# Gated unit's last weights: from 13 rows on every partition and one row dealt over five DMA engines to 12 rows and two rows dealt in stacks of four

## The chip, the cores and the metric

The kernel runs on one core of a Trainium2 chip. The metric is device time in microseconds (us), the median of several runs of the whole program. The engines are named as in the profile: PE (matrix multiplication; PEld its weight loads), DVE (vector), ACT (scalar), POOL (general), SP (here it issues nearly all transfers). "DMA engine" is one of the core's 16 transfer engines, which carry what SP and ACT issue.

## The reference

One decoding step for a batch of 8 with one token each, width 512. The token is normalised, then goes two ways: through attention over the last 2048 positions of a key and value cache (32 query heads, 8 cached heads of 128), and through a gated unit of width 1792. Both results are multiplied and added to the input.

```python
xn = _layernorm(x)
# A: attention over the last W = 2048 cached positions
q = (xn @ wq) as 32 heads of 128
scores = q . k * 128 ** -0.5 ;  p = softmax(scores) ;  o = p . v
s = o.reshape(B, 1, 4096) @ wo
# B: the gated unit
h = sigmoid(xn @ w_gate) * (xn @ w_up)
g = silu(h @ w_down)
return x + s * g
```

All arrays are bf16. `w_down` has 1792 rows of 512, 1 KB each, 1.79 MB in all. The cache windows are 64 MB, all weights together some 15 MB.

## The kernel before

The kernel is a long stream of loads with the arithmetic beside it. SP's queue loads the input and the weights of the gated unit (`wg_sb`, `wu_sb`), the query weights (`wq_sb`, two loads), `w_down`, then 16 tiles of keys and 16 of values of 2 MB each, alternating, and at the end the five pieces of `wo` (12, 8, 6, 4 and 2 rows on each partition). ACT issues two early loads: half of `wg_sb`, and the input in blocks (`x4_sb`, called `x_sb` in the profile).

What may be loaded when is set by a list and by room. `later` (L107) appends a load, `pump` (L110) issues loads from the head of the list while their pool has room, `free` (L116) gives a buffer back and pumps. There are five buffers of kind "k" (keys, `wq`, `wo`) and four of kind "v" (values, `wg`, `wu`, `w_down`). The order on every engine is the order in which the code is written.

The gated unit's second half multiplies the hidden values `h` by `w_down`. The rows of `w_down` stand on the partitions as `(y r) n -> y (r n)`: partition y holds rows 14y to 14y+13, 14 KB in one piece. Of these, rows 1 to 13 of every partition come in one load of 128 partitions (`wd_sb`, L196, `SD` = 1). Row 0 of each partition, 128 rows in all, comes in three further loads into a tile `wd_part` of 64 partitions (L179 to L192), which POOL sets to zero first (L183): 60 rows to partitions 0 to 19 in three slots each, 60 rows to partitions 32 to 51, and 8 rows to partitions 52 to 59 in one slot. The source of each of these loads has an outermost size of 5, 5 and 4 (`a` in L184 to L190). The tile takes one of the four "v" buffers.

The hidden values must stand on the same partitions as the dealt rows. A selection matrix `sel_part` (L276 to L285, seven small copies on DVE) and three matmuls (L363) move them there, DVE copies the result to `hP_sb` (L371), and the product with `w_down` (L384) then has 13 matmuls on 128 partitions and three on at most 60, summed into four column groups. ACT copies the sums (L394), four matmuls add them up (L397), ACT takes the sigmoid (L407) and DVE the product (L411). Then the attention begins: PE transposes the key tiles (L477), DVE copies them out (L482), scores (L496), softmax, values (L593). The last `wo` rows are multiplied at L729, and DVE's two last operations (L744, L746) precede the store.

The two lines that set where a dealt row goes:

```python
PARTS = ((0, NA, 0, SX, 0, A), (Z, NA, 0, SX, SX * NA, A))
in_=src.rearrange("(y a) n -> a y n", a=a)[:, :, : SD * w.shape[1]],
```

Of the kernel before, what the change touches and what calls it, by code (L numbers as in the profile page):

```python
# [10 lines left out]
def kernel(  # L11
# [13 lines left out]
    nc = tc.nc  # L25
    P = 128
    B, _, D = A_x.shape
    _, Hkv, Sk, Dh = A_k_cache.shape
# [5 lines left out]
    FT = F // P  # L34
# [14 lines left out]
    bf16 = mybir.dt.bfloat16  # L49
# [9 lines left out]
    vpool = ctx.enter_context(tc.tile_pool(name="vpool", bufs=4))  # L59
    ktpool = ctx.enter_context(tc.tile_pool(name="ktpool", bufs=3))  # L60
    ppool = ctx.enter_context(tc.tile_pool(name="ppool", bufs=2))
    consts = ctx.enter_context(tc.tile_pool(name="consts", bufs=1))
# [11 lines left out]
    ps_m = ctx.enter_context(  # L74
        tc.tile_pool(name="ps_m", bufs=1, space=bass.MemoryType.PSUM)
    )
    ctx.enter_context(tc.manual_schedule())


# [1 line left out]
    q0, q1 = nc.sync, nc.scalar  # L81
    k_tiles = {}
    v_tiles = {}
    room = {"k": 5, "v": 4}
    pools = {"k": kpool, "v": vpool}

    def load_cache(cache, tag, b, i):
# [16 lines left out]
    weights = {}  # L104
    todo = []

    def later(tag, f):  # L107
        todo.append((tag, f))

    def pump():  # L110
        while todo and room[todo[0][0]] > 0:
            tag, f = todo.pop(0)
            room[tag] -= 1
            f()

    def free(tag):  # L116
        room[tag] += 1
        pump()

    def want_rows(name, w, tag, per, r0, r1):  # L120
        def f():
            t = load_rows(w, tag, per, r0, r1, name)
            for r in range(r0, r1):
                weights[(name, r)] = t[:, r - r0, :]

        later(tag, f)
# [13 lines left out]
    Z = 32  # L140
# [26 lines left out]

    A = 5  # L170
    SD = 1
    SX = 3
    HP = P // 2
    NA = 4 * A
    PARTS = ((0, NA, 0, SX, 0, A), (Z, NA, 0, SX, SX * NA, A))
    PARTS += ((Z + NA, P - 2 * SX * NA, 0, 1, 2 * SX * NA, 4),)
    d_room = []

    def want_part(w, per):  # L179
        def f():  # L180
            d = vpool.tile([HP, SX, SD, w.shape[1]], bf16, name="wd_part", tag="v")
            d_room.append(d)
            nc.gpsimd.memset(d[:], 0.0)  # L183
            for p0, n, x0, x1, s0, a in PARTS:  # L184
                m = n * (x1 - x0)
                src = w.rearrange("(y r) n -> y (r n)", r=per)[s0 : s0 + m]
                q0.dma_start(
                    out=d[p0 : p0 + n, x0:x1].rearrange("p x r n -> p (x r n)"),
                    in_=src.rearrange("(y a) n -> a y n", a=a)[:, :, : SD * w.shape[1]],
                )  # L190

        later("v", f)  # L192

    for i in range(2):
        want_rows("wq_sb", A_wq, "k", KT, 2 * i, 2 * i + 2)
    want_rows("wd_sb", B_w_down, "v", FT, SD, FT)  # L196
    want_part(B_w_down, FT)
    order = [(b, i) for b in range(B) for i in range(NQ)]
    AHEAD = 3
# [5 lines left out]
    for t0, t1 in ((0, 12), (12, KS), (KS, 26), (26, 30), (30, RT)):  # L205
# [4 lines left out]
    ident = consts.tile([P, P], bf16, name="ident")  # L210
# [6 lines left out]
        out=perm[:].rearrange("k (l p) -> k l p", l=G),  # L217
        in_=ident[:].rearrange("k (p l) -> k l p", l=G),
# [13 lines left out]
        out=rstd[:], in_=mv[:, 1:2], func=AF.Sqrt, bias=eps_t[:], scale=1.0  # L232
# [4 lines left out]
        out=xn_bf[:],  # L237
# [8 lines left out]
    for kt in range(KT):  # L246
        nc.tensor.transpose(  # L247
            out=xnT_ps[:, kt, :],
            in_=xn_bf[:].rearrange("b (p kt) -> b kt p", kt=KT)[:, kt, :],
# [11 lines left out]
    for t in p_buf:  # L261
        nc.vector.memzero(t[:])
    oP_sb = work.tile([P, RT, Z], bf16, name="oP_sb")
    nc.vector.memzero(oP_sb[:])

    NDQ = Dh // RT
    own_q = consts.tile([P, NDQ], f32, name="own_q")
    nc.vector.reduce_sum(
        out=own_q[:], in_=ident_f[:].rearrange("k (h q) -> k q h", q=NDQ), axis=AX.X
    )  # L270
    sel_z = consts.tile([P, Z], f32, name="sel_z")
    nc.vector.reduce_sum(
        out=sel_z[:], in_=ident_f[:].rearrange("k (j z) -> k z j", z=Z), axis=AX.X
    )

    sel_part = consts.tile([P, SX, HP], bf16, name="sel_part")  # L276
    nc.vector.memzero(sel_part[:])
    for p0, n, x0, x1, s0, a in PARTS:
        for x in range(x0, x1):
            nc.vector.tensor_copy(  # L280
                out=sel_part[:, x, p0 : p0 + n].rearrange("k (a e) -> k a e", a=a),
                in_=ident[:, s0 : s0 + n * (x1 - x0)].rearrange(
                    "k (e x a) -> k x a e", x=x1 - x0, a=a
                )[:, x - x0],
            )  # L285

    FC = F // NB

    def hidden(name):
# [21 lines left out]
        out=h_sb[:].rearrange("k t p -> k p t"),  # L313
# [5 lines left out]
    hT_sb = work.tile([P, FT, Z], bf16, name="hT_sb")  # L319
    nc.vector.transpose(  # L320
        out=hT_sb[:].rearrange("k t z -> k (t z)"),
        in_=h_sb[:].rearrange("k t p -> k (t p)"),
# [4 lines left out]
    for kt in range(KT):  # L327
        for x in range(Hkv // JQ):
            for j in range(JQ):
# [5 lines left out]
                    start=(kt == 0),  # L335
                    stop=(kt == KT - 1),
                    tile_position=(0, Z * j),
                    skip_group_check=True,
# [3 lines left out]
    for x in range(Hkv // JQ):  # L342
        src = q_ps[x][:].rearrange("k (r d) -> k r d", r=rep)
# [4 lines left out]
    for x in range(Hkv // JQ):  # L348
        for r in range(rep):
            nc.tensor.transpose(  # L350
                out=qT_ps[:, x, r, :], in_=q_bf[:, x, r, :], identity=ident[:]
            )
        nc.vector.tensor_copy(
            out=qm_sb[:, :, x * JQ : (x + 1) * JQ, M0 : M0 + rep],
            in_=qT_ps[:, x].rearrange("d r (j z) -> d z j r", z=Z)[:, ::S],
# [2 lines left out]
    free("k")  # L358
    free("k")

    hP_ps = ps_t.tile([HP, SX, SD * Z], f32, name="hP_ps", tag="t")
    for x in range(SX):
        nc.tensor.matmul(  # L363
            hP_ps[:, x, :],
            lhsT=sel_part[:, x, :],
            rhs=hT_sb[:, :SD, :].rearrange("p t z -> p (t z)"),
            start=True,
            stop=True,
        )
    hP_sb = work.tile([HP, SX, SD * Z], bf16, name="hP_sb")  # L370
    nc.vector.tensor_copy(out=hP_sb[:], in_=hP_ps[:])  # L371
    down = [(hT_sb[:, t, :], weights[("wd_sb", t)]) for t in range(SD, FT)]
    for x in range(SX):
        top = max(p0 + n for p0, n, x0, x1, _, _ in PARTS if x0 <= x < x1)
        down += [
            (hP_sb[:top, x, Z * r : Z * (r + 1)], d_room[0][:top, x, r, :])
            for r in range(SD)
        ]


    w_ps = ps_s.tile([P, D], f32, name="w_ps", tag="s")
    for t, (h, w) in enumerate(down):
# [5 lines left out]
            start=(t < NB),  # L388
            stop=(t >= len(down) - NB),
            tile_position=(0, Z * j),  # L390
            skip_group_check=True,
# [4 lines left out]
    for j in range(NB):  # L396
# [4 lines left out]
            start=True,  # L401
            stop=True,
            tile_position=(0, Z * j),
            skip_group_check=True,
        )
    sigb = work.tile([P, P], f32, name="sigb")
    nc.scalar.activation(out=sigb[:], in_=b_ps[:], func=AF.Sigmoid)  # L407
    free("v")
    free("v")
    gg_sb = work.tile([P, P], f32, name="gg_sb")  # L410
    nc.vector.tensor_tensor(out=gg_sb[:], in0=sigb[:], in1=b_ps[:], op=ALU.mult)  # L411
# [5 lines left out]
    for i in range(NQ):  # L417
        nc.vector.tensor_copy(
            out=turn_rows[:].rearrange("k (i j l r) -> k i j l r", i=NQ, j=NJ, l=G)[
                :, i  # L420
            ],
            in_=ident[:].rearrange("k (l j i r) -> k i j l r", i=NQ, j=NJ, l=G)[:, i],
        )
        nc.vector.reduce_sum(
            out=sel_den[:, i * Hh : (i + 1) * Hh].rearrange("k (l r) -> k l r", l=G),
            in_=ident_f[:].rearrange("k (l j i r) -> k i l r j", l=G, j=NJ, i=NQ)[:, i],
            axis=AX.X,
        )
    for e in range(2):
        nc.vector.reduce_sum(  # L430
            out=sel_out[:, e, :].rearrange("k (i h) -> k i h", i=NQ),
            in_=ident_f[:].rearrange(
                "k (i m e h) -> k e i h m", i=NQ, m=NJ // 2, e=2
            )[:, e],
# [6 lines left out]

    sel_res = consts.tile([P, Hq, NDQ], f32, name="sel_res")
    nc.vector.tensor_tensor(
        out=sel_res[:],
        in0=sel_out[:, 0, :].unsqueeze(2).to_broadcast([P, Hq, NDQ]),
        in1=sel_out[:, 1, :].unsqueeze(2).to_broadcast([P, Hq, NDQ]),
        op=ALU.add,
    )
    sel_sum = consts.tile([P, Hq, NDQ], f32, name="sel_sum")
    nc.vector.tensor_copy(  # L450
        out=sel_sum[:], in_=sel_den[:].unsqueeze(2).to_broadcast([P, Hq, NDQ])
# [261 lines left out]
    for t in range(KS):  # L713
# [5 lines left out]
            start=(t < NB),  # L719
            stop=(t >= KS - NB),  # L720
            tile_position=(0, Z * j),
            skip_group_check=True,
# [16 lines left out]
    for t in range(KS, RT):  # L739
# [8 lines left out]
        out=out.flatten_outer_dims().rearrange("b (j c) -> j b c", c=P),  # L748
        in_=y_bf[::S, :],
# [31 lines left out]
```

## Time and profile before

| what | value |
|---|---|
| median of 3 runs | 199.63 us (199.55 to 199.66) |
| the profiled execution, whole | 199.53 us |
| its span, first to last instruction | 197.8 us |
| PE busy | 155.3 us, 79% |
| DVE busy | 122.7 us, 62% |
| ACT busy | 37.6 us, 19% |
| POOL busy | 3.0 us, 2% |
| moved by DMA | 81.32 MB, 411 GB/s on average |
| mean DMA rate from 60 to 120 us | 430 GB/s |
| `wd_sb`, issue to landing | 1664 KB, 22.1 us |
| `k_sb`, issue to landing (16) | 2048 KB, 32.1 us |
| `v_sb`, issue to landing (16) | 2048 KB, 27.3 us |

The span is cut into 40 equal slices on the page; a digit there is the busy share in tenths. A row of the window view has the window, its length, the busy time of PE, PEld, DVE, ACT and POOL with the number of their instructions, PE's granted clock as a share of the full one, the mean busy share of the 16 DMA engines, and GB/s. A row of the timeline has start, duration, engine, line, operation, output and inputs, count, and in brackets the idle time before it with what ended it. Beside the views, the trace keeps one record for each DMA packet: start, duration, queue and bytes, without the number of its DMA engine.

### The profile page before, as it was taken

The numbers are of one execution on the slowest core, as the hardware profiler recorded it, in microseconds if no ns is written. First come the engines' busy times: TensorE is split into PE (matmuls) and PEld (weight loads), VectorE is DVE, ScalarE is ACT, GpSimd is POOL, SyncE is SP. The second block draws the span as 40 slices with busy tenths as digits, with TensorE's granted clock in tenths as the row PEclk, the third lists the DMA queues.
The fourth block names the chain that finished last, engine by engine and source line by source line (L and its number), as shares of the span: only waits on it lengthen the run. The fifth ranks groups of instructions, "written<-read, shape, count | busy, mean of one in ns | idle before, by whom it ended". The sixth has DMA issues, their size and how long they took to land.

```text
span 197.8 us, 4771 instructions
## 1 busy us (share of the span) xinstructions
PE 155.3 (79%) x2133; PEld 104.6 (53%) x2133; DVE 122.7 (62%) x234; ACT 37.6 (19%) x91; POOL 3.0 (2%) x11
## 2 busy tenths in 40 slices
PE   0433576999799897979798959996999797888652
PEld 0111126676676574656565646674658464566421
DVE  3763117899798586748675927586858674752301
ACT  3300110001700500230024000600060023082010
POOL 6000000000000000000000000000000000000000
PEclk9999999999999999999999988999999999999955
DMA  5999999999999999999999999999999999999980
GB/s 213 437 444 431 414 444 424 427 424 426 434 424 434 441 417 431 421 441 421 431 434 426 427 427 437 419 434 431 427 424 434 421 441 421 441 424 423 411 348 16
DMA packets 6441, 81.32 MB, mean 411 GB/s; under 512 B 782, under 2 KB 918, under 8 KB 1558
## 3 DMA queue, kind: packets, MB, share of 16 engines
q1 hardware_dynamic: 6242, 80.10, 95.1%
q10 hardware_dynamic: 180, 0.93, 1.3%
q8 instruction: 16, 0.26, 0.5%
q14 instruction: 3, 0.02, 0.0%
HBM read 81.02 MB, written 0.01 MB: 410 GB/s over the span
## 4 chain that ended last, share of the span: by engine, by line
DMA 76%; PE 21%; SPq 1%; issue 0%; DVE 0%; POOL 0%; POOLq 0%
DMA k_sb<-in_A_k_cache_dram 61%; PE kT_ps L477 13%; DMA wo_sb<-in_A_wo_dram 11%; PE o_ps L593 4%; DMA x_sb<-in_A_x_dram 4%; PE s_ps L496 3%; SPq L99 1%; PE fin_ps L729 1%; PE pT_ps L567 0%; DVE prod L744 0%; PE m_ps L531 0%; DVE y_bf L746 0%; POOL wd_part L183 0%; PE m_ps L514 0%; POOL x_sb L144 0%
## 5 line engine op out<-in xcount | busy, mean ns | idle before, releaser
L482 DVE COPY kT_sb<-kT_ps 128x1024 bf16<-128x1024 bf16 x128 | 85.5, 687 | 35.1 <-PE kT_ps L477 34.4
L477 PE MATMUL kT_ps<-perm,k_sb 128*128 128x128 bf16 x1024 | 77.3, 224 | 14.4 <-DMA k_sb<-in_A_k_cache_dram 14.4
L477 PEld LDWEIGHTS <-k_sb 128*128 128x128 bf16 x1024 | 60.4, 100 | 35.0 <-DMA k_sb<-in_A_k_cache_dram 17.9
L593 PE MATMUL o_ps<-v_sb,pT_sb 128*32 128x256 bf16 x512 | 39.8, 277 | 1.1 <-DVE o_sb L614 0.9
L593 PEld LDWEIGHTS <-pT_sb 128*32 128x32 bf16 x512 | 21.9, 96 | 9.7 <-issue 3.2
L496 PE MATMUL s_ps<-kT_sb,qm_sb 128*32 128x512 bf16 x256 | 25.9, 395 | 0.7 <-DVE kT_sb L482 0.7
L544 ACT ACTIVATE p_buf<-s_ps,nb 32x512 bf16<-32x512 f32 x32 | 21.7, 679 | 0.5
L537 ACT COPY nb<-m_ps 128x1 f32<-128x1 f32 x8 | 1.3, 160 | 89.9 <-PE m_ps L531 89.9
L567 PE MATMUL pT_ps<-turn_rows,p_buf 128*128 128x128 bf16 x128 | 10.9, 230 | 1.5 <-ACT p_buf L544 1.5
L560 DVE COPY pT_sb<-pT_ps 128x1024 bf16<-128x1024 bf16 x14 | 9.6, 687 | 3.9 <-PE pT_ps L567 3.9
L567 PEld LDWEIGHTS <-p_buf 128*128 128x128 bf16 x128 | 9.3, 150 | 3.4 <-ACT p_buf L544 2.1
L496 PEld LDWEIGHTS <-qm_sb 128*32 128x32 bf16 x256 | 6.6, 93 | 7.8 <-issue 1.4
L331 PE MATMUL q_ps<-wq_sb,xnT_sb 128*32 128x512 bf16 x32 | 3.8, 626 | 6.2 <-DMA wq_sb<-in_A_wq_dram 6.2
L609 ACT ACTIVATE o_odd<-o_ps,own_col 128x128 f32<-128x128 f32 x8 | 2.9, 368 | 28.7 <-PE o_ps L593 28.6
L544 ACT ACTIVATION_READ_ACCUMULATOR p_buf<-s_ps,nb 32x1 f32 x32 | 5.9, 184 | 0.0
L331 PEld LDWEIGHTS <-xnT_sb 128*32 128x32 bf16 x32 | 1.3, 130 | 8.6 <-issue 8.6
L511 DVE TENSOR_REDUCE st<-s_ps 128x1 f32<-128x512 f32 x8 | 5.5, 682 | 0.5 <-PE s_ps L496 0.5
L347 DVE CAST q_bf<-q_ps 128x512 bf16<-128x512 f32 x1 | 0.7, 692 | 7.1 <-PE q_ps L331 7.1
L636 DVE SCALAR_TENSOR_TENSOR own<-m_ps,inv,own_q 128x128 f32<-128x128 f32 x8 | 2.8, 345 | 3.1 <-PE m_ps L627 3.1
L614 DVE SCALAR_TENSOR_TENSOR o_sb<-o_ps,own_col,o_odd 128x128 f32<-128x128 f32 x8 | 2.7, 340 | 3.0 <-ACT o_odd L609 3.0
L247 PE MATMUL xnT_ps<-ident,xn_bf 8*128 8x8 bf16 x4 | 0.3, 176 | 5.4 <-DVE xn_bf L236 5.4
L295 PE MATMUL h_ps<-wu_sb,xnT_sb 128*32 128x448 bf16 x16 | 1.7, 572 | 3.3 <-DMA wu_sb<-in_B_w_up_dram 3.3
(80 smaller groups left out, 62.9 us busy)
## 6 DMA issues: line engine op xcount, KB each, us to landing
k_sb<-in_A_k_cache_dram SPq DMA_DIRECT2D x16, 2048.0 KB, 32.1
v_sb<-in_A_v_cache_dram SPq DMA_DIRECT2D x16, 2048.0 KB, 27.3
wq_sb<-in_A_wq_dram SPq DMA_DIRECT2D x2, 2048.0 KB, 16.7
wu_sb<-in_B_w_up_dram SPq DMA_DIRECT2D x1, 1792.0 KB, 10.2
wd_sb<-in_B_w_down_dram SPq DMA_DIRECT2D x1, 1664.0 KB, 22.1
wo_sb<-in_A_wo_dram SPq DMA_DIRECT2D x1, 1536.0 KB
wo_sb<-in_A_wo_dram SPq DMA_DIRECT2D x1, 1024.0 KB, 20.0
wg_sb<-in_B_w_gate_dram ACTq DMA_DIRECT2D x1, 896.0 KB
```

The lines of the kernel that those rows point to most:

```text
L331: nc.tensor.matmul(q_ps[x][Z * j : Z * (j + 1), :], lhsT=xnT_sb[:, kt, :], rhs=weights[("wq_sb", kt)][:, g * rep * Dh : (g + 1) * rep * Dh ...
L477: nc.tensor.transpose(out=kT_ps[:, c, :], in_=k_sb[:, j * CU + h * CH + c, :], identity=perm[:],)
L482: nc.vector.tensor_copy(out=kT[(b, u)][:, h * CH : (h + 1) * CH, :], in_=kT_ps[:])
L496: nc.tensor.matmul(s_ps[b][NR * l : NR * (l + 1), :], lhsT=qm_sb[:, b, i * G + l, o : o + Z], rhs=t[:, :, PG * l : PG * (l + 1)], start=(u ...
L511: nc.vector.reduce_max(out=st[b][:], in_=s_ps[b][:], axis=AX.X)
L544: nc.scalar.activation(out=p_buf[b % 2][rows, :, l, :], in_=s[rows, :].rearrange("k (c p) -> k p c", p=PG), func=AF.Exp, bias=nb[rows, :], ...
L560: copy(out=pT[b][:, h * CH : (h + 1) * CH, :], in_=pT_ps.pop(h)[:])
L567: nc.tensor.transpose(out=pT_ps[h][:, c, :], in_=p_buf[b % 2][:, :, :, h * CH + c].rearrange("k p l -> k (p l)"), identity=turn_rows[:],)
L593: nc.tensor.matmul(o_ps[rows, b % 2, :].rearrange("k (e d) -> k e d", e=2), lhsT=pT[b][:, c, rows], rhs=v[:, m, c], start=(c == 0), stop=( ...
L609: nc.scalar.mul(out=o_odd[:], in_=o_ps[:, b % 2, Dh:], mul=own_col[:, 1:2])
L614: nc.vector.scalar_tensor_tensor(out=o_of[b // 2][:, b % 2, :], in0=o_ps[:, b % 2, :Dh], scalar=own_col[:, 0:1], in1=o_odd[:], op0=ALU.mul ...
L636: nc.vector.scalar_tensor_tensor(out=own[:], in0=m_ps[:, b % 2, P : 2 * P].rearrange("p (q t) -> p q t", q=NDQ), scalar=inv[y][:, b % 2 : ...
```

## The change

Two rows of every partition are now dealt instead of one (`SD` = 2), so `wd_sb` holds 12 rows on each of the 128 partitions. The other 256 rows come as 128 pairs of 2 KB into a tile `d_part` of 40 partitions with four slots each (`SX` = 4): 96 pairs to partitions 0 to 23 by a load whose source has an outermost size of 6, and 32 pairs to partitions 32 to 39 by one with an outermost size of 2. The tile has a pool of its own, so it takes no "v" buffer; DVE sets its first 32 partitions to zero as DVE's first operation, where POOL did it before. The selection matrix takes two larger copies instead of seven, selection four matmuls instead of three, and the product 12 matmuls on 128 partitions and eight on 40. The numbers of rows multiplied and bytes of weights loaded do not change.

```diff
-    room = {"k": 5, "v": 4}
+    room = {"k": 5, "v": 4, "d": 1}
...
-    A = 5
-    SD = 1
-    SX = 3
-    HP = P // 2
-    NA = 4 * A
-    PARTS = ((0, NA, 0, SX, 0, A), (Z, NA, 0, SX, SX * NA, A))
-    PARTS += ((Z + NA, P - 2 * SX * NA, 0, 1, 2 * SX * NA, 4),)
-    d_room = []
+    SD = 2
+    SX = 4
+    SHARES = ((0, 6, 0), (Z, 2, 24 * SX))
+    HP = Z + 8
+    d_part = d_pool.tile([HP, SX, SD, D], bf16, name="wd_part")
+    nc.vector.memzero(d_part[:Z])
...
-            d = vpool.tile([HP, SX, SD, w.shape[1]], bf16, name="wd_part", tag="v")
-            d_room.append(d)
-            nc.gpsimd.memset(d[:], 0.0)
-            for p0, n, x0, x1, s0, a in PARTS:
-                m = n * (x1 - x0)
-                src = w.rearrange("(y r) n -> y (r n)", r=per)[s0 : s0 + m]
+            for p0, a, s0 in SHARES:
+                n = 4 * a
+                src = w.rearrange("(y r) n -> y (r n)", r=per)[s0 : s0 + n * SX]
                 q0.dma_start(
-                    out=d[p0 : p0 + n, x0:x1].rearrange("p x r n -> p (x r n)"),
-                    in_=src.rearrange("(y a) n -> a y n", a=a)[:, :, : SD * w.shape[1]],
+                    out=d_part[p0 : p0 + n].rearrange("p x r n -> p x (r n)"),
+                    in_=src.rearrange("(y a) n -> a y n", a=a)[
+                        :, :, : SD * w.shape[1]
+                    ],
                 )
-        later("v", f)
+        later("d", f)
...
+    sel_part = consts.tile([P, SX, HP], bf16, name="sel_part")
+    nc.vector.memzero(sel_part[:])
+    for p0, a, s0 in SHARES:
+        n = 4 * a
+        nc.vector.tensor_copy(
+            out=sel_part[:, :, p0 : p0 + n].rearrange("k x (a p) -> k x a p", a=a),
+            in_=ident[:, s0 : s0 + n * SX].rearrange(
+                "k (p x a) -> k x a p", x=SX, a=a
+            ),
+        )
...
+    down += [
+        (hP_sb[:, x, Z * r : Z * (r + 1)], d_part[:, x, r, :])
+        for x in range(SX)
+        for r in range(SD)
+    ]
...
     nc.scalar.activation(out=sigb[:], in_=b_ps[:], func=AF.Sigmoid)
     free("v")
-    free("v")
```

## The prediction

> **What bounds the kernel now.** I read the page first. The DMA row is full in 37 of 40 slices, and the chain that ended last is 76% DMA.
>
> ```profile
> span 197.8 us, 4771 instructions
> ...
> DMA  5999999999999999999999999999999999999980
> ...
> q1 hardware_dynamic: 6242, 80.10, 95.1%
> ...
> q8 instruction: 16, 0.26, 0.5%
> q14 instruction: 3, 0.02, 0.0%
> ...
> DMA 76%; PE 21%; SPq 1%; issue 0%; DVE 0%; POOL 0%; POOLq 0%
> ```
>
> So the transfers set the time. Nearly all is on SP's queue (q1); two small queues (q8, q14) fetch instructions through the same 16 DMA engines. Next I cut the end into windows. The last two columns are the mean busy share of the 16 DMA engines and GB/s:
>
> ```profile
> 189.50:190.50 1.00, 0.40 (x5) 0.13 (x7) 0.00 (x0) 0.00 (x0) 0.00 (x0) 0.50 0.99 410
> 190.50:191.25 0.75, 0.65 (x8) 0.00 (x0) 0.00 (x0) 0.06 (x1) 0.00 (x0) 0.50 0.80 325
> 191.25:192.00 0.75, 0.17 (x4) 0.17 (x8) 0.00 (x0) 0.53 (x1) 0.00 (x0) 0.50 0.63 257
> 192.00:192.75 0.75, 0.75 (x28) 0.69 (x28) 0.00 (x0) 0.00 (x0) 0.00 (x0) 0.50 0.56 224
> 192.75:193.00 0.25, 0.25 (x16) 0.19 (x6) 0.00 (x0) 0.00 (x0) 0.00 (x0) 0.50 0.57 221
> 193.00:193.25 0.25, 0.14 (x11) 0.01 (x3) 0.00 (x0) 0.00 (x0) 0.00 (x0) 0.50 0.28 107
> 193.25:193.50 0.25, 0.25 (x12) 0.25 (x15) 0.00 (x0) 0.00 (x0) 0.00 (x0) 0.50 0.09 33
> ```
>
> The engines do not stop together: seven run dry between 190.3 and 192.0, and 0.56 is 9 of 16 still working to 193.0. These nine gain nothing from the others' rest: 224 GB/s over nine is 25 each, against 27 each (428 over 16) in mid-kernel. Each DMA engine thus has a pace of its own, and **the slowest engine's bytes and stalls set the end**.
>
> For the rest I went to the trace's packet records (start, duration, queue, bytes; no engine named). A 16 KB packet always takes 611 ns and its successor starts 607 ns after it, so sixteen chains can be followed from 11 us to the end. Three facts come out. (a) The three `wd_part` transfers ran on 5, 5 and 4 chains, the outermost sizes of their sources, nested: four chains carry all three, a fifth the first two. (b) The 16 q8 fetches fall on eight other chains, two each; a fetch and the packet it shares the engine with cost that chain 1.42 us, so 2.83 to 2.85 us each. (c) The three q14 fetches (8 KB) fall on two of the four: one chain, X, takes two (1.68 us), one, Y, takes one (0.55 us). The last packet of each chain, in us:
> - the eight: 193.03 to 193.50
> - the four: X 192.96, Y 191.99, the others 191.37 and 191.42
> - the fifth: 191.20
> - the remaining three: 190.27, 190.59, 190.60
>
> The last packet at 193.50 frees PE's last `wo` matmuls, and from there to the span's end only fixed work follows.
>
> **The change, part by part.**
>
> *One row fewer on all partitions.* Each engine carries eight `wd` packets of 12 instead of 13 KB. Packets of 16 KB follow each other by 607 ns and of 12 KB (`wo`) by 456, so 38 ns per KB: 8 x 38 = **-0.30 us on every engine**. Nothing else comes to the eight if the new transfers go elsewhere.
>
> *The dealt rows.* Out go 26 packets of 1 KB on the four and 24 on the fifth, 42 to 43 ns each: from the last `wd` packet to the first `k` packet 1.12 and 1.03 us. In come 16 packets of 2 KB for each outermost step, and a 2 KB packet (`wo`, rows 30 to 32) takes 80 ns: 1.29 us with the end mark. By (a) six chains get this once, two of them twice. Per chain:
> - the eight: -0.30, to 192.73 to 193.19
> - two of the four, once: -0.30 - 1.12 + 1.29 = -0.13
> - two of the four, twice: -0.30 - 1.12 + 2.57 = +1.15
> - fifth: -0.30 - 1.03 + 1.29 = -0.04
> - a sixth, taken as one of the three: -0.30 + 1.29 = +0.99, to at most 191.6
>
> Doubled, an undisturbed one of the four ends at 191.42 + 1.15 = 192.57 and Y at 193.14, both before 193.19; X would end at 194.11. X with a single share ends at 192.83. **If X is not doubled, the eight still end last and the sum is -0.30 us.** Which of the four are doubled no row says.
>
> One rule of the Trainium skill speaks against the change: "DMA: Bandwidth & Descriptors", Rules for kernel authors, asks for an outermost size that is a multiple of 16, since a smaller one confines the transfer to that many engines. By that rule the six and the two are the fault, and the sum would be rival D's; the windows above, with seven engines idle at the end, speak against that here. Another section, "Runtime: NRT & Kernel Launch", Instruction fetch mechanics, calls the cost of a 16 KiB instruction block mostly hidden; the trace differs, with 1.42 us on the DMA engine that fetches it.
>
> *PE.* One `wd` matmul and three `wd_part` matmuls go, eight `wd_part` matmuls and one selecting matmul come: five more in all, ten rows with the weight loads. That is short of a further instruction block: PE ran 256 or so between fetches and 194 after the last.
>
> ```profile
> 27.38 0.61 PE L384 MATMUL w_ps<-wd_part,hP_sb 60*32 60x512 bf16 x3
> ...
> 31.23 3.59 PE L477 MATMUL kT_ps<-perm,k_sb 128*128 128x128 bf16 x32 [1.89 <-DMA k_sb<-in_A_k_cache_dram]
> ```
>
> The doubled chains deliver their rows at about 24.5 + 2.57 = 27.1, usable some 0.4 later, so PE waits 0.1 to 0.2 at the first `wd_part` matmul; five further ones at 0.2 add 1.0. The 1.89 us that PE then waits for `k_sb` hide this. But the first `k_sb` itself lands with the slowest of the four (last packet 30.85): +1.15, so PE starts its first tile near 32.4. I cost this at nothing: k tiles are issued 32 us before they land, v tiles 27, so late releases leave the queue full. Without that cover it would cost up to 1.15.
>
> *SP, POOL, DVE, ACT.* With two part transfers instead of three and no v buffer for them, SP issues the `k` and first `v` loads one semaphore turn earlier; 15 us of transfers stand ahead of them: nothing. POOL loses a 1.38 us memset. DVE gains one of 32x2048 words in front of its first copy: by `qm_sb`'s 128x1920 in 1.66 about 1.77 us, over by some 2.5, and the copy starts at 2.79; if it came later, up to 1 us is hidden, since PE waits for `wg_sb` to 7.62. Seven small selection copies (0.74 us) become two; `hP_sb` grows from 96 to 256 columns (0.25 us, at most 0.5 by `q_bf`'s 512 in 0.69). SP's first part issue now waits for DVE's memset in place of POOL's, with all `k` and `v` issues behind it; SP comes to it at 5.52, 3 us after the memset. All lie before 31 us, beside the transfers. ACT's issues do not move.
>
> **The sum.** Profiled execution: 199.53 us, 197.8 of it span; 199.53 - 0.30 = 199.23. The median of the three timed runs, 199.63, is 0.10 above this execution, so I forecast 199.63 - 0.30 = **199.33 us**. Two sizes are open. Y doubled, with a fetch that costs 0.84 (X's mean) in place of 0.55, ends at 193.43: the gain shrinks to 0.07. And PE runs the tail at a granted clock of 0.50 from 188.9; its last 8 matmuls take 0.43 us, so a full clock there would save 0.2 more. So 199.1 to 199.6 in this case.
>
> **The rivals.**
> - **B, the doubled pair holds X.** Mechanism: 64 KB on the chain that also loses 1.68 us to fetches; it decides as soon as that chain's last packet passes 193.19. 194.11 instead of 193.50: +0.62, **200.25 us, slower**. For it: the pair is nested in the four, and three of the six pairs hold X. I put it somewhat below a half, as a judgement.
> - **C, the sixth chain is one of the eight.** Then it ends 0.99 later than now, at 194.0 to 194.5: 200.2 to 200.6. Against it: the eight with two fetches each look like one block, and eight chains are without.
> - **D, the engines end level in an unprofiled run**, the fetches being spread otherwise. Then the doubled pair is last: +1.15, 200.8. Against it: the windows.
> - **E, the change does not do what it says**: the sources spread over all 16 engines. 256 KB is 16 KB on each, 0.61 to 0.64 us, less 0.30: +0.3 on the eight, 199.95. Against it: 5, 5 and 4 chains now.
>
> **Chances.** Forecast 0.57 (0.20 of it below 199.23), B 0.28, C 0.07, D 0.04, E 0.04. Taking 0.2% (0.40 us, about what a measurement of this kernel can tell from no change) as the border: faster 0.20; same 0.37 + 0.03 of B at full clock + 0.04 of E = 0.44; slower 0.25 + 0.07 + 0.04 = 0.36. The range takes in the forecast and B: 199.1 to 200.3; the forecast alone 199.1 to 199.6.
>
> **What would show it.** After the change, `wd` packets 456 ns apart; 2 KB packets on six chains, on two of them 32; the window before the end with about eight to ten engines busy and none after 193.2; PE's first `kT_ps` near 32.4; the span 0.3 us shorter. If one engine works alone after 193.3, B or C holds, and whether that chain has q14 or q8 fetches tells which. If the DMA row shows a gap in mid-kernel, my cover for the late first tile was wrong.

## The result and the profile after

The changed kernel takes 200.01 us in the median of 13 runs (199.81 to 200.40), the kernel before 199.59 (199.44 to 199.96) in the same comparison. The ratio is 1.0020, 95% interval 1.0012 to 1.0029: **slower by 0.2%**, 0.42 us by the medians, where the forecast was 0.30 us faster. The profiled execution took 199.92 us, 0.39 more than the one of before.

The page of the changed kernel, the same lines as before:

```profile
span 198.0 us, 4775 instructions
...
DMA  6999999999999999999999999999999999999980
...
q8 instruction: 16, 0.26, 0.5%
q14 instruction: 3, 0.02, 0.0%
...
DMA 76%; PE 20%; SPq 1%; issue 0%; DVE 0%
```

The transfers still set the time, the queue has no gap in mid-kernel, and the number of instruction fetches is the same (16 and 3). The windows of the end (last two columns: share of the 16 DMA engines at work, GB/s):

```profile
192.00:192.75 0.75, 0.54 (x13) 0.48 (x17) 0.00 (x0) 0.16 (x1) 0.00 (x0) 0.50 0.59 232
192.75:193.00 0.25, 0.25 (x20) 0.25 (x16) 0.00 (x0) 0.00 (x0) 0.00 (x0) 0.50 0.23 90
193.00:193.25 0.25, 0.25 (x20) 0.25 (x13) 0.00 (x0) 0.00 (x0) 0.00 (x0) 0.50 0.20 74
193.25:193.50 0.25, 0.25 (x12) 0.08 (x1) 0.00 (x0) 0.00 (x0) 0.00 (x0) 0.50 0.06 25
193.50:193.75 0.25, 0.18 (x11) 0.17 (x12) 0.00 (x0) 0.00 (x0) 0.00 (x0) 0.50 0.06 25
193.75:194.00 0.25, 0.25 (x16) 0.25 (x9) 0.00 (x0) 0.00 (x0) 0.00 (x0) 0.50 0.02 8
```

The reader is to see the 0.06 in two whole windows: that is 1 of 16, **one DMA engine working alone** at its own 25 GB/s, while fifteen are done. Before, nine stopped close together. The packet records give the last packet of each chain (the chains are again told apart by what they carry; "sixth" is the one that the outermost size of 6 adds), in us:

| chain | before | forecast | after |
|---|---|---|---|
| the eight with two q8 fetches, without dealt rows | 193.03 to 193.50 | 192.73 to 193.19 | seven: 192.40 to 193.24 |
| X (two q14 fetches), rows once | 192.96 | 192.83 | 192.77 |
| Y (one q14 fetch), rows twice | 191.99 | 193.14 | 193.17 |
| the other doubled one | 191.37 or 191.42 | 192.57 | 192.47 |
| the other two of the first five | 191.20; 191.37 or 191.42 | 191.16 to 191.29 | 191.06, 191.42 |
| sixth | not told apart | at most 191.6 | **193.83** |
| three without fetches and rows | 190.27 to 190.60 | 190.0 to 190.3 | 189.71 to 190.47 |

X is not doubled, as the forecast had wished. But the sixth chain is not one of the three free ones: it carries two q8 fetches, each with its loss of 1.42 us, and the dealt rows on top. That is the sign which the prediction named for rival C: one engine alone after 193.3, with q8 fetches. So the eight are seven chains without dealt rows and the sixth, and the three free chains lie on engines that no dealt row reaches.

PE went as forecast. Three rows of the timeline:

```profile
1.22 1.76 DVE L176 MEMSET wd_part<- 32x2048 uint32 x1 [1.22 <-PEq L760]
...
27.61 1.04 PE L380 MATMUL w_ps<-wd_part,hP_sb 40*32 40x512 bf16 x8 [0.41 <-DMA wd_part<-in_B_w_down_dram]
...
32.42 3.29 PE L472 MATMUL kT_ps<-perm,k_sb 128*128 128x128 bf16 x32 [2.43 <-DMA k_sb<-in_A_k_cache_dram]
```

The memset ends at 2.98, the eight `wd_part` matmuls wait 0.41 for their rows, and the first key tile starts 1.19 us later than before.

### The profile page after: what moved, and what is told of

Read it like the earlier page. It is cut to its first block, busy times and chain, and to the rows that moved or that the text cites. A ratio compares the mean times of both kernels' runs of the same rounds, so it can differ in the third digit from the quotient of the medians.

```text
span 198.0 us, 4775 instructions
## 1 busy us (share of the span) xinstructions
PE 155.3 (78%) x2138; PEld 104.3 (53%) x2138; DVE 124.2 (63%) x230; ACT 37.6 (19%) x91; POOL 3.0 (1%) x10
## 4 chain that ended last, share of the span: by engine, by line
DMA 76%; PE 20%; SPq 1%; issue 0%; DVE 0%
DMA k_sb<-in_A_k_cache_dram 62%; PE kT_ps L472 12%; DMA wo_sb<-in_A_wo_dram 11%; PE o_ps L588 4%; DMA wg_sb<-in_B_w_gate_dram 3%; PE s_ps L491 3%; SPq L100 1%; PE fin_ps L724 1%; PE pT_ps L562 0%; SPq L150 0%; DVE prod L739 0%; PE m_ps L526 0%; DVE y_bf L741 0%; PE m_ps L509 0%; SPq L90 0%
```

## The experiments

First I held the doubled pair to be at fault, as in rival B: **theory 1**. **Theory 2**: the late first key tile delays PE for good. **Theory 3**: the cost lies outside the engines' loads. Each edit is against the changed kernel. A comparison's ratios are to the kernel before, timed with it on the same chip: 199.75 us (33 runs) for the first four experiments, 199.45 us (27 runs) for the last three.

| run | median us | ratio to before (95%) | last packet, and which chain |
|---|---|---|---|
| changed kernel | 200.01 | 1.0020 (1.0012 to 1.0029) | 193.83 sixth |
| e1, one transfer over eight | 200.09 | 1.0017 (1.0008 to 1.0026) | 193.85 and 193.79, two of the sixth to eighth; 193.63, without dealt rows |
| e2, no second transfer | 200.15 | 1.0016 (1.0007 to 1.0025) | 194.34 sixth |
| e4, 15 pairs in the second | 200.00 | 1.0015 (1.0007 to 1.0024) | 194.14 sixth |
| e5, 128 memsets more on DVE | 200.02 | 1.0015 (1.0006 to 1.0023) | 194.09 sixth |
| e8, over five and three | 199.29 | 0.9990 (0.9981 to 0.9999) | 193.14, Y |
| e9, five in place of six | 199.14 | 0.9985 (0.9977 to 0.9994) | 193.21, X |
| e10, no dealt rows | 199.29 | 0.9991 (0.9982 to 1.0000) | 193.18, one of the eight |

**e1_eight.**

```diff
-    SHARES = ((0, 6, 0), (Z, 2, 24 * SX))
-    HP = Z + 8
+    SHARES = ((0, 8, 0),)
+    HP = Z
```

> All 128 pairs are dealt by one transfer with an outermost size of 8 to partitions 0 to 31, so no chain is doubled. Theory 1 (the doubled pair holds X, the chain that also carries two q14 fetches): the eight chains with the q8 fetches end last again, 0.30 us earlier than before: 199.3 us, 0.7 under the changed kernel; X's last packet near 192.6 to 192.9. Theory 2 (the doubled chains make the first k tile late and PE's work never catches up): 199.3 too, since the first tile comes as early as before. Theory 3 (something else of the change costs: DVE's memset in front, the wider selection, the own pool): 200.0, as the changed kernel.

Nothing was gained. The windows of its end:

```profile
193.00:193.25 0.25, 0.25 (x21) 0.25 (x13) 0.00 (x0) 0.00 (x0) 0.00 (x0) 0.50 0.20 74
193.25:193.50 0.25, 0.25 (x12) 0.10 (x4) 0.00 (x0) 0.00 (x0) 0.00 (x0) 0.50 0.19 74
193.50:193.75 0.25, 0.19 (x12) 0.15 (x11) 0.00 (x0) 0.00 (x0) 0.00 (x0) 0.50 0.15 57
```

0.19 is three of sixteen engines: three chains run on to 193.63, 193.79 and 193.85. All three carry two q8 fetches. The last two carry dealt rows as well; the one that ends at 193.63 carries none, but its `wd` load ended only at 25.33, 0.5 us after that of any other q8 chain. X, with a single share, is done by about 193.1. So theory 1 and theory 2 fall (the first key tile starts at 31.27, as early as before).

The eight chains with dealt rows are X, Y, four without any fetch, and these two. The first five engines hold X, Y and three without fetches. So of the sixth, seventh and eighth engine two belong to the eight and one is free; e2 shows next that the sixth belongs to the eight.

**e2_six_only.**

```diff
-    nc.vector.memzero(d_part[:Z])
+    nc.vector.memzero(d_part[:])
...
-            for p0, a, s0 in SHARES:
+            for p0, a, s0 in SHARES[:1]:
```

> The second transfer of dealt rows (32 pairs over two engines) is left out, and its partitions are zero; 64 of the 1792 rows of w_down are thus missing from the product, all instructions stay. Theory 1: 199.3 us, X's last packet near 192.5, the eight last at 193.2. Theory 2: 199.3. Theory 3: 200.0.

No chain is doubled, and yet one engine works alone for about a microsecond:

```profile
193.25:193.50 0.25, 0.25 (x16) 0.22 (x9) 0.00 (x0) 0.00 (x0) 0.00 (x0) 0.50 0.04 16
193.50:193.75 0.25, 0.17 (x8) 0.00 (x0) 0.00 (x0) 0.00 (x0) 0.00 (x0) 0.50 0.06 25
193.75:194.00 0.25, 0.00 (x0) 0.00 (x0) 0.00 (x0) 0.00 (x0) 0.00 (x0) 0.50 0.06 25
194.00:194.25 0.25, 0.17 (x9) 0.17 (x12) 0.00 (x0) 0.00 (x0) 0.00 (x0) 0.50 0.06 25
```

It is the sixth chain, again with two q8 fetches. PE's columns show the price: it stands idle from 193.7 to 194.1 for the last rows of `wo`.

**e4_engine0.**

```diff
-    nc.vector.memzero(d_part[:Z])
+    nc.vector.memzero(d_part[:])
...
-            for p0, a, s0 in SHARES:
+            for p0, a, s0 in SHARES[:1]:
...
+            src = w.rearrange("(y r) n -> y (r n)", r=per)[96:111]
+            q0.dma_start(
+                out=d_part[Z : Z + 5, :3].rearrange("p x r n -> p x (r n)"),
+                in_=src.rearrange("(u v) n -> u v n", u=3)[:, :, : SD * w.shape[1]],
+            )
```

> The second transfer is replaced by one of 15 pairs with sizes 5 and 3 outermost, so that all of it runs on one engine, the lowest; the other 17 pairs are left out and the 15 stand in other places than the selection expects, so the product is changed. One chain alone carries 31 packets of 2 KB. Theory 1: if that chain is the one with two q14 fetches (X), 199.9 to 200.0 us as the changed kernel and its last packet near 193.8; if X is the other of the pair, 199.3. Theory 2: 200.0 whichever it is, since the first k tile is late by 1.1 us in both cases. Theory 3: 200.0.

This one missed its aim: the transfer ran on five engines, three packets each (eleven end marks for the dealt rows, six of them from the first transfer), so no chain carried 31 packets. It decides nothing on X. It is one more run in which the sixth chain ends alone, at 194.14.

**e5_ticks.**

```diff
+    tick = consts.tile([1, 1], f32, name="tick")
...
             k_transposes(b, s // 2, s % 2)
+            nc.vector.memset(tick[:], 0.0)
```

> The changed kernel with 128 further one-element memsets on DVE, one after each half tile of keys, so that DVE passes one more block of instructions. Theory 1 with X's fetches being DVE's: four q14 fetches before 195 us in place of three, the added one on the doubled chain X, which costs it 0.84 us more: 200.8 us. If X's fetches are another engine's: 200.0, and the added fetch on another chain. Theory 2 and 3: 200.0 to 200.1, as DVE is busy for 62% only and the transfers stay as they are.

The time did not move against the other variants. The page shows the added fetch:

```profile
q8 instruction: 16, 0.26, 0.5%
q14 instruction: 4, 0.03, 0.0%
```

Chain X now takes three, at 41.6, 94.1 and 158.7 us, and loses 0.84 us by each. The fetch that DVE's memsets added is on X, so X's fetches are DVE's. But X is not doubled and ends at 193.76, before the sixth chain's 194.09. That half of theory 1 that names X's fetches holds; the half that makes X the last one does not.

**Theory 4**, formed from these four: the sixth engine is one of those that fetch PE's instructions, and its dealt rows put it last and alone.

**e8_five_three**, which deals all rows without the sixth engine:

```diff
-    SHARES = ((0, 6, 0), (Z, 2, 24 * SX))
-    HP = Z + 8
+    SHARES = ((0, 5, 0), (Z, 3, 20 * SX))
+    HP = Z + 12
```

> All rows are dealt, 80 pairs over five engines (partitions 0 to 19) and 48 over three (partitions 32 to 43), so that no engine beyond the fifth gets any. Theory 4 (formed after the first four experiments: the sixth chain is one of the eight with q8 fetches, and its 1.29 us of dealt rows put it last and alone): the eight end together again at 193.2 and the time is 199.3 to 199.4 us, 0.3 under before, unless X is among the three that are doubled; then X is alone at about 194.0 and the time 200.1 to 200.2. Theory 3 (something else of the change costs, whatever the engines carry): 200.0 to 200.1, as all variants so far.

It computes the whole product and beats both kernels: 0.9990 of before, 199.29 us. All sixteen engines are done by 193.2:

```profile
192.75:193.00 0.25, 0.20 (x12) 0.16 (x11) 0.00 (x0) 0.00 (x0) 0.00 (x0) 0.50 0.33 123
193.00:193.25 0.25, 0.25 (x16) 0.25 (x9) 0.00 (x0) 0.00 (x0) 0.00 (x0) 0.50 0.03 8
193.25:193.50 0.25, 0.23 (x12) 0.04 (x8) 0.00 (x0) 0.00 (x0) 0.00 (x0) 0.50 0.00 0
```

X is not among the three doubled chains either (it ends at 192.85).

**e9_no_sixth**, which differs from the changed kernel in the sixth engine's load alone:

```diff
-    SHARES = ((0, 6, 0), (Z, 2, 24 * SX))
+    SHARES = ((0, 5, 0), (Z, 2, 20 * SX))
```

> The changed kernel with five in place of six engines in the first transfer: five chains carry 16 packets, two of them 32, the sixth none; 16 of the 128 pairs are left out (32 of 1792 rows of w_down hold old bytes in the product). Only the sixth chain's load differs from the changed kernel. Theory 4: no single chain after 193.3, 199.3 to 199.4 us, 0.6 to 0.7 under the changed kernel. Theory 3: 200.0 to 200.1.

With two chains still doubled and only the sixth relieved, the ratio goes from 1.0020 to 0.9985, and no engine works alone:

```profile
192.75:193.00 0.25, 0.08 (x5) 0.08 (x8) 0.00 (x0) 0.00 (x0) 0.00 (x0) 0.50 0.30 115
193.00:193.25 0.25, 0.25 (x16) 0.25 (x16) 0.00 (x0) 0.00 (x0) 0.00 (x0) 0.50 0.09 33
193.25:193.50 0.25, 0.25 (x12) 0.09 (x4) 0.00 (x0) 0.00 (x0) 0.00 (x0) 0.50 0.00 0
```

Its first key tile starts at 32.49, as late as in the changed kernel (32.42): a second ground against theory 2. DVE's memset, the wider selection and the own pool are all still in it: theory 3 falls.

**e10_none.**

```diff
-    nc.vector.memzero(d_part[:Z])
+    nc.vector.memzero(d_part[:])
...
-            for p0, a, s0 in SHARES:
+            for p0, a, s0 in SHARES[:0]:
```

> No dealt row is loaded: both transfers are left out and their tile is zero, so 256 of 1792 rows of w_down are missing from the product; all other instructions stay. Theory 4: the eight set the end alone, 199.3 to 199.4 us as with five engines: the dealt rows cost nothing while they stay off the eight and off X. Theory 3: 200.0.

0.9991, and 199.29 us, the same median as e8. Taking all dealt rows away gains nothing over dealing them to the first five engines.

## Why the prediction was wrong, point by point

- **The bound: right.** The slowest DMA engine sets the end. In the profiled executions the last packet moved by +0.34 us (193.50 to 193.83), the issue of the final store by +0.35 (194.96 to 195.30), the whole by +0.39. The span of the profile grew by 0.17 only (197.80 to 197.97); what shortened the stretch after the store's issue stays open.
- **One row fewer, -0.30 us on every engine: not contradicted.** e8, e9 and e10, where the eight carry no dealt rows, lie 0.16, 0.31 and 0.16 us under before. The intervals are some 0.17 us wide on each side, so the runs don't settle 0.30 more closely.
- **The cost of the dealt rows: right in size.** 80 ns for a packet of 2 KB; from the last `wd` packet to the first `k` packet 1.29 us on a single chain and 2.57 on a doubled one.
- **The step that failed** is the line "a sixth, taken as one of the three: -0.30 + 1.29 = +0.99, to at most 191.6". I took the eight as one block beyond the first eight engines, with the three free chains as number six to eight. No row said so. The changed kernel, e2, e4 and e5 show the sixth with two q8 fetches, last at 193.83 to 194.34 where the line had at most 191.6; by e1 only one of the sixth to eighth is free, and the other two free ones lie beyond. Relieved of its dealt rows (e9), the sixth no longer ends alone, and the time falls below that of before. What I had as rival C, with 0.07, is what happened, and I had no better ground for 0.07 than that the eight look like a block. Of the eleven chains without dealt rows before, eight were fetching ones: by count alone C had 8 in 11.
- **C's size: a little too high.** I gave 200.2 to 200.6, from a last packet at 194.0 to 194.5; it was 193.83 here and, for a chain of the eight with dealt rows, 193.79 to 194.34 in e1, e2, e4 and e5. The chains start in another order in each execution: the last packets of the eight spread over 0.47 us before and those of the seven without dealt rows over 0.84 after, and I took one execution's spread for fixed. In the changed kernel's profiled execution the sixth was one of the first two of the eight to end its `wd` load.
- **B: wrong.** X is not among the doubled two, nor among the three of e8. The 200.01 us lie inside the wide range of 199.1 to 200.3 by luck: its upper part was there for B, which did not happen, and C's price lay mostly outside it.
- **D and E: wrong.** The transfers ran on six and two engines (eight end marks), and the engines don't end level. A rule of the Trainium skill bears on this: "DMA: Bandwidth & Descriptors", Rules for kernel authors, asks for an outermost size that is a multiple of 16. No run here deals the rows over 16 engines, so the rule itself is not tried; but five and three engines gave 0.9990 and eight 1.0017, so here it counted more which engines carried the rows than how many. The same page, in the section on why a DMA increments its semaphore by 16, says that a transfer of k < 16 engines takes the lowest-numbered k; the nesting of the 5, 5 and 4, the 6 and 2 and the 5 and 3 chains agrees with it.
- **PE, DVE, POOL: right.** The first key tile at 32.42 (forecast 32.4), the five further matmuls within the 1.0 us forecast, the memset 1.76 (forecast 1.77), the fetches still 16. The wait at `wd_part` was 0.41 instead of 0.1 to 0.2. All of it stayed hidden.

## What to carry to other kernels

Where transfers fill the whole span, cut the end into windows fine enough to count the DMA engines still at work, and give extra bytes only to engines that are shown to finish early. An engine's number isn't in the packet records, so a plan that loads "one engine more" must first be tried for which chain it lands on, by a transfer with that outermost size (here e2 for six). Where a guess about identity carries the sign of the forecast, its chance is the count of the cases, not how tidy one of them looks.

## What the runs showed of the hardware

- Instruction fetches cost the DMA engine that makes them more than their bytes: 1.42 us for the 16 KB blocks of q8, where a 16 KB packet of the kernel takes 0.61, and 0.84 us for DVE's 8 KB blocks on X. Y's one fetch of 8 KB costs 0.55. That q8's blocks are PE's is taken from the count (before, 222 to 312 recorded instructions of PE lie between two fetches, 258 on average); no run tries it. The Trainium skill ("Runtime: NRT & Kernel Launch", Instruction fetch mechanics) calls the cost of a block mostly hidden; here it is not hidden from the transfers.
- The q8 blocks go in turn over eight DMA engines, two each in this kernel. In the order in which transfers take engines, none of the first five is among them, the sixth is, and so is one of the seventh and eighth (e1). DVE's blocks all come through one engine, X, one of the first four; e5's added fetch came there too.
- Loads taken off the slow engines by 0.30 us (0.15%) came out as a gain of 0.1 to 0.15% in the whole; 16 small packets on one wrong engine (32 KB of 81 MB) cost more than that.
